# A new table of issue order, engines and TensorE fillers for an attention-and-feed-forward kernel on one Trainium2 core

## The chip, the core and the metric

The kernel runs on one core of a Trainium2 chip. A core has five instruction streams, each strictly in order: TensorE (PE, with its weight loads shown apart as PEld), VectorE (DVE), ScalarE (ACT), GpSimd (POOL) and SyncE (SP), which issues nearly all DMAs. [...] The metric is the device time of one execution in microseconds; the time before is 741.42 us, the median of three runs (740.2 to 742.83).

## The reference

Attention over 4 batches, 8 heads, 576 positions and 64 dimensions a head, with a bias that a small network makes from the relative position (the same for all batches), and then a two-layer feed-forward part on the 2304 x 512 result.

```python
scores = scale * np.matmul(q, k.transpose(0, 1, 3, 2))
x = (psi_rel / psi_i)[..., None]               # log1p(|i-j|) / log1p(max(i,1))
bias = np.maximum(x @ w1 + b1, 0.0) @ w2       # 32 hidden units, 8 heads
attn = softmax(scores + bias)                  # over the last axis
out = np.matmul(attn, v)                       # -> x of (B*S, H*D) = (2304, 512)
h = x @ w_in                                   # d_ff = 2048
g = np.maximum(h, 0.0) + alpha * np.minimum(h, 0.0)
return g @ w_out
```

## The kernel before, in words

The program is made in two steps. First the functions below record 2816 work items, each with its engine alternatives (an item may be able to run on ACT, DVE or POOL), its operands and its buffers. Then `plan` reads three tables of numbers. `ISSUE` gives the order in which the items are issued, and behind a dot the alternative that each takes (`58.2` is item 58 on its third alternative). `SLOT` gives the buffer of each tile. `IDLE` (`62:24`) says that 24 fillers stand ahead of item 62: matmuls of 512 columns on zeros into the tile `H`, which nobody reads (L995). Nothing is decided at run time: each engine runs its items in the table's order, and an item that has to wait holds up all that stands behind it on its engine. The framework sets the semaphores from the tiles that the items touch, in the table's order.

What runs, in time:

- **Bias tiles** (`bias_tile`, 36 of them, until about 130 us). Four "H" items each make max(R*sign + psi, 0) on 128 partitions and 304 to 576 columns, on ACT (L479), DVE (L476) or POOL (L482). PE multiplies them with `w2b` into PSUM (L497), one item scales the result into `fg` (L507 or L508), and SP writes it to DRAM (`scr`).
- **Weights** (`weights`, 8 pairs of blocks, mixed with the bias tiles). DVE puts 32-bit halves together (L667, L670), takes a maximum (L674), and both weights are split into a high and a low 16-bit part (L695, L696, L689, L690, and L388 on DVE for the low part). Two tiny PE transposes (L458, L460) spread each maximum over all partitions.
- **Attention units** (`unit`, 64 of them). SP loads the bias rows into `fg`; PE makes scores (L602 in 32 bits for batch 0, L603 in three 16-bit products for batches 1 to 3); DVE adds the bias and takes the row extremum (L797); ACT exponentiates (L800); the sums are inverted (L803, L805). In batch 0 the rows are then scaled (L820 on POOL, L821 on DVE) and turned on PE (L829, copied back by L839 or L840). In batches 1 to 3 a high part (item "nh", L810 on POOL or L811 on ACT) and a low part (L813 on DVE) go into one of two `a` buffers, and two DMA transposes on SP write them to `at`. PE multiplies with v (L850, L858), and ACT and DVE write the two parts of `x` (L876, L878).
- **Feed-forward chunks** (`chunk`, `layer_pair`; 9 chunks of 256 rows, 8 pairs of hidden blocks each, from 195.7 us on). The first layer is 24 matmuls (L928) into the one `H` buffer; ACT (L935) and DVE (L936) apply the activation; item "g0" (L939) and item "g1" (L940 on DVE, L941 on POOL) split the result; the second layer is 12 matmuls (L947) that add up in PSUM tile `O`, one half for each 128 rows. The last pair of a group issues the two halves of `O` as two PE items of six matmuls, and each half is then evicted (item "mo", L909 on ACT or L910 on DVE; L913 on DVE where four groups are added up, in chunks 0 and 1).

The lines around the fillers are:

```python
    gaps = {int(n): int(k) for n, k in (x.split(":") for x in IDLE.split())}
    with tc.manual_schedule():
        for o in ordered:
            for _ in range(gaps.get(o.seq, 0)):
                nc.tensor.matmul(idle, lhsT=zero.broadcast_to((P, P)), ...)
            o.alt()
```

## Time and profile before

| | |
|---|---|
| median of three runs | 741.42 us |
| the profiled execution | 740.16 us, span 738.3 us (first to last instruction) |
| PE busy | 678.8 us (92%), 5712 matmuls |
| DVE busy | 534.7 us (72%) |
| ACT busy | 366.5 us (50%) |
| POOL busy | 239.8 us (32%) |
| mean granted PE clock | 0.988 |

Until 195.7 us no feed-forward matmul runs; this stretch is called the first stage below, the rest the second. Busy time is the union of an engine's instructions; PE's includes the fillers. In the first nine of the page's forty slices PE stands at 7 to 8 tenths mostly and DVE at 9, and from slice 11 on PE stands at 9 and DVE at 6 to 8. PE's clock is granted in full from about 160 us on.

### The profile page before, as it was taken

The page shows a single profiled execution, that of the slowest core. Times are in us where ns is not written, and L with a number is a line of the kernel's source. Part 1 is how long each engine was busy: PE and PEld are TensorE (multiplying, and loading weights), DVE is VectorE, ACT ScalarE, POOL GpSimd, SP SyncE. Part 2 cuts the span into 40 slices and gives each one's busy share as a digit, 9 for nine tenths or more (in the row PEclk, how much of TensorE's full clock was granted, in tenths as well). Part 3 has the DMA queues.
Part 4 walks back from the last instruction along what each step waited for, and adds up shares of the span by engine and source line. Part 5 has one row for each costly group of instructions (what it writes and reads, how often), then busy time and mean ns, then how long its engine had stood idle before and what let it go on. Part 6 is the DMA issues. An engine that isn't in the chain of part 4 may idle for free. (4 is left out here: it accounts for less than half of the span.)

```text
span 738.3 us, 15339 instructions
## 1 busy us (share of the span) xinstructions
PE 678.8 (92%) x5712; PEld 425.4 (58%) x5712; DVE 534.7 (72%) x1228; ACT 366.5 (50%) x753; POOL 239.8 (32%) x297
## 2 busy tenths in 40 slices
PE   7777779787999989998999999999999999999997
PEld 3444334444665656665667565656666666666764
DVE  6999899999687879898778766767676656333322
ACT  3556657566565547664465564544454534211221
POOL 2556677523122313233322232224223232110110
PEclk9999989899999999999999999999999999999999
DMA  8897875773849888999999998788789965400000
GB/s 204 212 285 258 257 278 183 243 207 120 211 107 229 177 185 174 218 209 223 194 229 199 173 206 177 163 194 211 138 178 199 193 143 84 68 29 1 29 1 29
DMA packets 236554, 125.89 MB, mean 171 GB/s; under 512 B 204864, under 2 KB 204864, under 8 KB 236480
## 3 DMA queue, kind: packets, MB, share of 16 engines
q1 hardware_dynamic: 233840, 124.90, 72.3%
q8 instruction: 45, 0.74, 0.4%
q10 hardware_dynamic: 2640, 0.01, 0.2%
q14 instruction: 29, 0.24, 0.1%
HBM read 73.87 MB, written 15.61 MB: 121 GB/s over the span
## 5 line engine op out<-in xcount | busy, mean ns | idle before, releaser
L947 PE MATMUL O<-wout,mg 128*128 128x512 f16 x864 | 199.0, 379 | 8.4 <-DVE mg L910 3.4
L928 PE MATMUL H<-x,win 128*128 128x256 f16 x1728 | 200.7, 273 | 2.8 <-DVE mg L936 2.7
L928 PEld LDWEIGHTS <-win 128*128 128x128 f16 x1728 | 166.8, 98 | 35.0 <-issue 8.5
L935 ACT ACTIVATE mg<-H,sm 128x256 f32<-128x256 f32 x144 | 65.0, 471 | 155.7 <-PE H L928 122.5
L947 PEld LDWEIGHTS <-mg 128*128 128x128 f16 x864 | 82.1, 98 | 103.3 <-issue 13.7
L800 ACT ACTIVATE fg<-fg,st 128x576 f32<-128x576 f32 x144 | 110.8, 770 | 59.7 <-DVE st L797 52.1
L936 DVE SCALAR_TENSOR_TENSOR mg<-H,sm,mg 128x256 f32<-128x256 f32 x144 | 67.0, 480 | 95.6 <-ACT mg L935 95.1
L813 DVE SCALAR_TENSOR_TENSOR a<-fg,st,a 128x576 f16<-128x576 f32 x108 | 97.9, 909 | 26.6 <-POOL a L810 16.1
L810 POOL TENSOR_SCALAR a<-fg,st 128x576 f16<-128x576 f32 x74 | 59.9, 811 | 175.3 <-DMA at<-a 72.9
L941 POOL TENSOR_TENSOR mg<-mg 128x512 f16<-128x512 f32 x48 | 61.2, 1275 | 151.6 <-DVE mg L939 51.1
L797 DVE CUSTOM_DVE_ANT_0 fg<-S,fg 128x576 f32<-128x576 f32 x127 | 93.4, 749 | 20.6 <-PE S L603 19.7
L482 POOL TENSOR_SCALAR at<-cst,npsi 128x496 f32<-128x496 f32 (+16 forms) x66 | 56.2, 860 | 45.7 <-PE S L497 30.2
L497 PE MATMUL S<-at,w2b 128*32 128x79 f32 (+37 forms) x684 | 54.4, 355 | 15.7 <-POOL at L482 7.0
L603 PE MATMUL S<-qk 64*128 64x288 f16 (+1 forms) x678 | 52.8, 285 | 1.2 <-DVE st L797 0.9
L497 PEld LDWEIGHTS S<-at,w2b 128*32 128x32 f32 x684 | 26.3, 114 | 46.0 <-POOL at L482 18.5
L850 PE MATMUL A<-at,five 128*64 128x256 f16 (+3 forms) x720 | 51.6, 288 | 0.0
L603 PEld LDWEIGHTS <-qk 64*128 64x128 f16 (+1 forms) x720 | 32.1, 96 | 23.7 <-issue 18.1
L850 PEld LDWEIGHTS <-five 128*64 128x64 f16 (+1 forms) x720 | 36.1, 109 | 14.5 <-issue 11.3
L803 POOL TENSOR_SCALAR st<-st 128x2 f32<-128x2 f32 (+1 forms) x42 | 13.3, 316 | 80.2 <-ACT fg L800 70.3
L811 ACT ACTIVATE a<-fg,st 128x576 f16<-128x576 f32 x34 | 26.3, 773 | 14.3 <-DMA at<-a 4.9
L820 POOL TENSOR_SCALAR fg<-fg,st 128x576 f32<-128x576 f32 x29 | 24.9, 864 | 24.2 <-DVE st L805 12.9
L479 ACT ACTIVATE at<-cst 128x576 f32<-128x576 f32 (+16 forms) x39 | 24.8, 655 | 15.8 <-PE S L497 11.5
(148 smaller groups left out, 825.9 us busy)
## 6 DMA issues: line engine op xcount, KB each, us to landing
fg<-scr SPq DMA_DIRECT2D x64, 576.0 KB, 4.7
scr<-fg SPq DMA_DIRECT2D x36, 295.5 KB, 4.4
x<-in_moe_w_in_dram SPq DMA_DIRECT2D x10, 512.0 KB, 5.7
x<-in_moe_w_out_dram SPq DMA_DIRECT2D x10, 512.0 KB, 4.5
fg<-scr SPq DMA_DIRECT2D x32, 144.0 KB, 4.5
out_dram<-mg SPq DMA_DIRECT2D x18, 256.0 KB, 2.9
five<-in_q_dram SPq DMA_DIRECT2D x32, 128.0 KB, 4.3
five<-in_k_dram SPq DMA_DIRECT2D x32, 128.0 KB, 4.0
```

The lines of the kernel that those rows point to most:

```text
L497: nc.tensor.matmul(ps.t[32 * gl:32 * gl + 32, c:n], lhsT=w2b, rhs=x, start=True, stop=True)
L603: return [(lambda a, dst=dst, zq=zq, zk=zk, i=i: nc.tensor.matmul(dst(a), lhsT=tr16(qt)[at, 0, pr, zq, lo:lo + n], rhs=tr16(qt)[at, 1, pr, ...
L797: V(lambda x=x, sl=sl, st=st, ls=ls: nc.vector.tensor_tensor_reduce(out=in_halves(ls[x]()), in0=halves(sl[x].t), in1=in_halves(ls[x]()), s ...
L800: A(lambda x=x, st=st, ls=ls: nc.scalar.activation(ls[x](), ls[x](), AF.Exp, bias=st.t[:, x:x + 1], scale=-1.0, accum_out=st.t[:, 2 + x:3 ...
L810: pl.op([("POOL", 775, lambda x=x, rec=rec, ls=ls, a16=a16: nc.gpsimd.tensor_scalar(a16.t[:, 0:S], ls[x](), rec(), 1.0, op0=ALU.mult, op1= ...
L813: V(lambda x=x, rec=rec, ls=ls, a16=a16: nc.vector.scalar_tensor_tensor(a16.t[:, 640:640 + S], ls[x](), rec(), a16.t[:, 0:S], op0=ALU.mult ...
L850: nc.tensor.matmul(ps.t[64 * hh:64 * hh + 64, 0:w], lhsT=v5[0:hi, zv, n, 2 * pr + hh, :], rhs=at16(at)[0:hi, 5 * za + n, 320 * hh:320 * hh ...
L928: nc.tensor.matmul(hb.t[:, f, :], lhsT=win[:, fp, zw, kb, P * f:P * f + P], rhs=x[:, zx, kb, :], start=(n == 0), stop=(n == 11))
L935: A(lambda f=f: nc.scalar.activation(gf(f), hb.t[:, f, :], AF.Copy, scale=cu[:, f:f + 1]), 470, ky, [hb, t_sig], [(g, f)])
L936: V(lambda f=f: nc.vector.scalar_tensor_tensor(gf(f), hb.t[:, f, :], cs[:, f:f + 1], gf(f), op0=ALU.mult, op1=ALU.max), 475, ky, [hb, t_si ...
L941: ("POOL", 1210, lambda: nc.gpsimd.tensor_tensor(gv(1), g.t, gv(0), op=ALU.subtract))], ky, [g, (gg, 0)], [(gg, 1)], tag="g1", cont=True)
L947: nc.tensor.matmul(ob.t[:, t, :], lhsT=gg.t[:, zg, f, P * t:P * t + P], rhs=wout[:, fp, zw, f, :], start=(first and f == 0 and (zg, zw) == ...
```

## The change

Only `ISSUE` and `IDLE` differ; the items, their arithmetic, the buffers (`SLOT`) and all code stay. The file is one line shorter, so every line number behind the tables is lower by one in the kernel after (L947 is L946 there).

```diff
 ISSUE = """
-11.1 15.1 3 9.1 0 203 2 12.1 1 204 205 206 17 14.1 8.1 5.1 19 20 21 22 24 6.1 23 25 29 58.2 59.2 61.1 16.1 207 80.2 13.1 10.1 7.1 33 26 60 62 208 209
...
+3 5.1 0 203 2 8.1 1 207 11.1 17 14.1 12 15.1 6.1 16.1 7.1 204 205 9.1 206 13.1 208 10.1 209 18.1 210 215 219 33 211 19 20 21 22 24 34 23 25 29 26 58
...
 IDLE = """
-62:24 118:1 111:2 683:3 97:3 655:2 132:2 641:1 676:3 957:1 139:3 634:1 697:1 160:3 669:2 146:2 725:2 704:3 711:1 753:1 739:2 746:3 569:2 767:2 560:1
-353:1 580:2 596:2 614:1 806:9 814:3 793:2
+30:23 62:2 118:2 90:1 104:1 111:2 683:2 55:3 97:3 132:1 641:2 676:4 959:1 662:1 139:2 634:2 697:1 160:2 669:4 718:5 725:4 704:1 711:1 739:7 388:1
+569:3 549:2 767:1 563:1 353:3 596:3 611:1 800:1 419:1 614:1 806:2 814:8 828:4 796:2
```

Counted in the two tables, 289 of the 2816 items run on another engine:

| items | before | after |
|---|---|---|
| on DVE / ACT / POOL / SP | 1084 / 602 / 293 / 423 | 1101 / 658 / 219 / 424 |
| H on ACT / DVE / POOL | 43 / 29 / 72 | 72 / 36 / 36 |
| nh on POOL / ACT | 74 / 34 | 65 / 43 |
| g1 on POOL / DVE | 48 / 24 | 33 / 39 |
| mo on DVE / ACT | 10 / 8 | 5 / 13 |
| of those that the first L928 item hangs on: DVE / ACT / POOL | 330 / 167 / 124 | 343 / 205 / 75 |
| fillers | 91 | 111 |
| places on PE where the tile shape of one item differs from the last | 318 (193 from the first L928 item on) | 324 (188) |

The row on the first L928 item counts the items that must be done before it: those that it depends on through data and buffers, and those that stand ahead of these on their engines. On PE the order moves little: 258 of the 414 items keep their place in the row, and none moves by more than five. All fillers stand in the first stage in both.

Three places show what moved. The first is DVE's start of the program, where L667, L670 and L674 belong to the first weight block, L422 to L426 scale the small network's first weights, and L427 to L432 prepare the constants that every H item reads. Before:

```order
L667 TENSOR_SCALAR win<-mg 128x512
L670 SCALAR_TENSOR_TENSOR win<-mg,win 128x512 x2
L422 TENSOR_REDUCE sm<-sm 128x1
L423 TENSOR_SCALAR sm<-sm 128x1
L424 RECIPROCAL sm<-sm 128x1
L425 TENSOR_TENSOR sm<-sm 128x1
L427 TENSOR_SCALAR cst<-cst,sm 128x576
L426 TENSOR_TENSOR sm<-sm 128x1
L428 TENSOR_SCALAR cst<-cst,sm 128x144
L432 TENSOR_SCALAR npsi<-cst 128x144
L476 TENSOR_SCALAR at_85<-cst 128x560
L429 TENSOR_SCALAR w2b<-w2b,sm 128x32
```

After:

```order
L666 TENSOR_SCALAR win<-mg 128x512
L669 SCALAR_TENSOR_TENSOR win<-mg,win 128x512 x2
L666 TENSOR_SCALAR win<-x_93 128x512
L669 SCALAR_TENSOR_TENSOR win<-x_93,win 128x512 x2
L673 TENSOR_REDUCE sm<-win 128x1
L421 TENSOR_REDUCE sm<-sm 128x1
L422 TENSOR_SCALAR sm<-sm 128x1
L423 RECIPROCAL sm<-sm 128x1
L424 TENSOR_TENSOR sm<-sm 128x1
L426 TENSOR_SCALAR cst<-cst,sm 128x576
L425 TENSOR_TENSOR sm<-sm 128x1
L427 TENSOR_SCALAR cst<-cst,sm 128x144
```

The second half of the first weight block (`x_93`) and its maximum now stand ahead of the small network's chain, and the H item (L476) behind it has gone. In the table SP's load of the constants has moved behind the load of `x_93`, and one of ACT's small loads is now issued by SP.

The second place is ACT in the first bias tiles (L479 and L478 are H items, L507 and L506 the scaling of a finished tile, L675 and L674 a weight's maximum). Before:

```order
L479 ACTIVATE fg<-cst 128x512
L479 ACTIVATE at_85<-cst 128x432
L507 ACTIVATE fg<-S_64,cst 128x591
L479 ACTIVATE at_85<-cst 128x432
L507 ACTIVATE fg<-S_65,cst 128x591
L507 ACTIVATE fg<-S_64,cst 128x591
L675 ACTIVATE wout,sm<-wout 128x1024
L479 ACTIVATE at_85<-cst 128x544
L479 ACTIVATE fg<-cst 128x400
L507 ACTIVATE fg<-S_64,cst 128x591
```

After:

```order
L478 ACTIVATE at_85<-cst 128x560 x2
L478 ACTIVATE fg<-cst 128x512
L478 ACTIVATE at_85<-cst 128x512
L506 ACTIVATE fg<-S_64,cst 128x591
L478 ACTIVATE at_85<-cst 128x432 x3
L478 ACTIVATE at_85<-cst 128x496
L478 ACTIVATE fg<-cst 128x496
L478 ACTIVATE at_85<-cst 128x496
L506 ACTIVATE fg<-S_65,cst 128x591
L674 ACTIVATE wout,sm<-wout 128x1024
```

Between two scalings there stood no more than two H items, and now up to six stand there; their counterparts have left POOL.

The third place is the end of the program on PE: the weight load and matmul that end the first half of the last chunk's `O`, and the start of the second half, with the semaphores that each waits for. Before:

```order
L947 LDWEIGHTS mg
L947 MATMUL O_63<-wout,mg 128x512
L947 LDWEIGHTS mg
L947 MATMUL O_63<-wout,mg 128x512 [waits DVE_49]
L947 LDWEIGHTS mg
```

After:

```order
L946 LDWEIGHTS mg
L946 MATMUL O_63<-wout,mg 128x512
L946 LDWEIGHTS mg
L946 MATMUL O_63<-wout,mg 128x512
L946 LDWEIGHTS mg
```

The eviction of the first half stood ahead of the second half's matmuls in the table and stands behind them now, and the wait for it has gone. In the same way an eviction stood between two halves in seven places before; in four of these nothing but the eviction stood between them for PE. Now it does so in two places (chunk 1, groups 0 and 1), with other PE items between.

## Rows read from the trace of the kernel before

**Rows 1.** Windows: length, busy us (count) of PE, PEld, DVE, ACT, POOL, PEclk, DMA.
```profile
0.00:20.00 20.00, 15.12 (x116) 7.19 (x116) 12.81 (x32) 7.21 (x9) 6.74 (x12) 0.91 0.87 201
20.00:180.00 160.00, 126.82 (x1209) 67.47 (x1208) 151.42 (x298) 97.12 (x169) 91.23 (x110) 0.96 0.73 230
180.00:196.00 16.00, 15.02 (x113) 9.13 (x112) 11.16 (x37) 8.18 (x20) 4.98 (x7) 1.00 0.79 196
196.00:560.00 364.00, 348.54 (x2974) 227.51 (x2973) 281.66 (x689) 199.56 (x436) 106.07 (x139) 1.00 0.90 189
560.00:738.30 178.30, 173.25 (x1310) 114.11 (x1306) 77.65 (x174) 54.44 (x122) 30.83 (x31) 1.00 0.35 74
```

**Rows 2.** Timeline of 4.5 to 13.5 us, DVE and POOL: start, length, idle before.
```profile
4.55 0.43 DVE L667 TENSOR_SCALAR win<-mg 128x512 int32<-128x512 int32 x1 [2.27 <-DMA mg<-in_moe_w_in_dram]
5.01 1.42 DVE L670 SCALAR_TENSOR_TENSOR win<-mg,win 128x512 int32<-128x512 int32 x2
...
8.24 0.15 DVE L422 TENSOR_REDUCE sm<-sm 128x1 f32<-128x1 f32 x1 [1.81 <-DMA sm<-in_w_dram]
...
10.32 1.62 POOL L482 TENSOR_SCALAR at<-cst,npsi 128x560 f32<-128x560 f32 x2 [9.88 <-DVE npsi L432]
...
11.92 0.95 POOL L482 TENSOR_SCALAR fg<-cst,npsi 128x512 f32<-128x512 f32 x1
...
12.34 1.07 DVE L670 SCALAR_TENSOR_TENSOR win<-x,win 128x512 int32<-128x512 int32 x1
```

**Rows 3.** Durations by line, ns min/median/max: L670, L482, L479, L476.
```profile
L670 DVE SCALAR_TENSOR_TENSOR five<-x,five x22: 680/693/1486, 96.2 to 173.6; 128x512 int32<-128x512 int32 x22
...
L482 POOL TENSOR_SCALAR at<-cst,npsi x66: 517/764/2063, 10.3 to 126.7; 128x544 f32<-128x544 f32 x5, 128x464 f32<-128x464 f32 x5, 128x384 f32<-128x384 f32 x5, 128x560 f32<-128x560 f32 x4
...
L479 ACT ACTIVATE at<-cst x39: 537/651/779, 10.0 to 129.3; 128x576 f32<-128x576 f32 x4, 128x416 f32<-128x416 f32 x4, 128x432 f32<-128x432 f32 x3, 128x544 f32<-128x544 f32 x3
...
L476 DVE TENSOR_SCALAR at<-cst x24: 373/494/929, 10.1 to 115.2; 128x496 f32<-128x496 f32 x3, 128x400 f32<-128x400 f32 x3, 128x480 f32<-128x480 f32 x3, 128x384 f32<-128x384 f32 x2
```

**Rows 4.** Windows of one line each, first stage: L670 and L476 (DVE), L482 (POOL).
```profile
0.00:196.00 196.00, 53.40 (x64) 0.96 0.75 225
...
0.00:196.00 196.00, 17.21 (x29) 0.96 0.75 225
...
0.00:196.00 196.00, 61.59 (x72) 0.96 0.75 225
```

**Rows 5.** Waits of PE from 196 us: in total, times, longest (us).
```profile
PE O L947 <- DVE mg L910: 3.4, 3, 1.8
PE H L928 <- DVE mg L936: 2.7, 4, 1.0
PE O L947 <- DVE mg L913: 2.0, 1, 2.0
```

**Rows 6.** Timeline where an eviction stands between two halves of `O`.
```profile
269.55 0.74 DVE L913 SCALAR_TENSOR_TENSOR mg<-O,sm,mg 128x512 f32<-128x512 f32 x1
...
270.35 1.46 PE L947 MATMUL O<-wout,mg 128*128 128x512 f16 x6 [2.00 <-DVE mg L913]
...
416.95 1.46 PE L947 MATMUL O<-wout,mg 128*128 128x512 f16 x6 [1.75 <-DVE mg L910]
...
732.98 1.46 PE L947 MATMUL O<-wout,mg 128*128 128x512 f16 x6 [0.84 <-DVE mg L910]
```

**Rows 7.** Timeline of PE: a first layer before another shape, and before its own.
```profile
586.59 2.79 PE L928 MATMUL H<-x,win 128*128 128x256 f16 x24
589.32 0.92 PE L603 MATMUL S<-qk 64*64 64x288 f16 x12
...
657.06 2.78 PE L928 MATMUL H<-x,win 128*128 128x256 f16 x24
659.68 2.54 PE L947 MATMUL O<-wout,mg 128*128 128x512 f16 x11
```

**Rows 8.** What POOL's "nh" items (L810) waited for: us, times.
```profile
  DMA at<-a: 72.9, 27
```

183 rows, old and new, of the table ISSUE are left out of this document.

## The prediction

> **What bounds the kernel now.** I read the windows by stage first [rows 1], then the start of the timeline [rows 2], then durations by line [rows 3], and for the later part the waits of PE [rows 5]. From 20 to 180 us DVE is busy for 151.42 of 160 us, while PE has 126.82, ACT 97.12 and POOL 91.23: in the first stage everybody waits for DVE, so this stage is priced as DVE's. From 196 us on it is the other way round: PE is busy for 348.54 of 364 us and then for 173.25 of 178.3, DVE for 281.66 of 364 (77%). There only what keeps PE from its next matmul counts. The reader is to see that PE's whole idle time from 196 us on is 15.5 + 5.0 us, and 33.2 us from 20 to 180.
>
> **First stage: DVE beside POOL.** The same instruction of DVE has two lengths. At 5.01 us two L670 take 1.42 us, 0.71 each, and POOL has nothing to do yet; at 12.34 one L670 takes 1.07 us, and POOL runs an H item of 0.95 us that began at 11.92 [rows 2]. Over the run L670 goes from 680 to 1486 ns [rows 3]. In the first stage its 64 instructions take 53.40 us [rows 4] against 64 x 0.68 = 43.5: 9.9 us are lengthening. For L476 (29 H items on DVE, 17.21 us) the widths differ, so I bound it: 29 x 0.494 (the median) leaves 2.9 us of lengthening, 29 x 0.373 (the shortest) leaves 6.4; I take 4.6, the middle. Of DVE's other lines that read SBUF I show no row; I put 1.5 us for them, and 16 us in all. POOL, which does this, is busy for 6.74 + 91.23 + 4.98 = 103 us in this stage. The change takes 49 of 124 items off it, 36 of them H items at 61.59 / 72 = 0.855 us [rows 4]; pricing all 49 so, 41.9 us of 103 go. In proportion DVE gets back 16 x 41.9 / 103 = 6.5 us. The ends are 0 (what is left of POOL stands in the way as often) and 16 (nothing meets any more).
>
> [...]
>
> **First stage: work that comes to DVE.** Of the items that the first L928 hangs on, DVE has 13 more. Seven are H items at 0.494 us [rows 3]: 3.5 us. The other six are the net of likes that come and go; between nothing and six mean instructions of this stage (175.4 us / 367 = 0.48, so 2.9 us) [rows 1]. I take 1.5; together +5.0 us.
>
> **First stage: the start.** Before, DVE waits for the first weight half (2.27 us) and then for the small network's weights (1.81 us, until 8.24) [rows 2]. Now the second weight half stands in that gap: one L667 and two L670 more (0.43 + 1.42 = 1.85 us) and a maximum, which I price at two L670 (1.42). So when the chain of L422 begins, at about 4.55 + 2 x 1.85 + 1.42 = 9.7 us instead of 8.24, DVE is 3.3 us of work ahead; the H items begin 1.4 us later. Net 1.8 us gained, about the 1.81 us of the gap. It needs the constants by then: SP's load of them now waits until the first weight half has landed (4.55 us), so it has 5 us; if it lands later, this term falls to 0. The small load that moves from ACT to SP waits behind that, and is needed at the same time.
>
> First stage: -6.5 + 5.0 - 1.8 = **-3.3 us**. Three things I cost at nothing. ACT takes 38 items more, 29 of them H items at 0.651 us [rows 3] (18.9 us): it has 62.9 us idle between 20 and 180 us; if that cover is gone it is a rival below. The 20 fillers more run in PE's 33.2 us of idle time. And SP's other loads only change places with neighbours.
>
> **Second stage: the evictions between two halves.** PE's longest waits there are not for data. The second half of a chunk's last item waits for the eviction of the first half, which stands ahead of it in the table: 3.4 us in three waits for L910 and 2.0 us in one for L913 [rows 5], at 270.35 (2.00), 416.95 (1.75), 732.98 and one more (0.84 each) [rows 6]. At 269.55 one sees why the first is so long: L913 itself starts late, since DVE does other work first. In the new order none of the four has an eviction between: -5.4 us. The 0.84 us at the end is sure, as nothing but the last eviction follows. For the others something is late next: behind the one at 270 the score item that reuses `O`'s bank has both evictions ahead of it (0 to 0.74 us; I take 0.5). The two places where an eviction now stands between have cover: in chunk 1, group 1, a whole first layer (2.6 us), so nothing; in group 0 only twelve score matmuls (0.92 us [rows 7]) and a small pair against an eviction of 0.74 us and what DVE has ahead of it: 0 to 2.0, the longest wait seen; I take 0.6. Together +1.1.
>
> **Second stage: changes of tile shape.** A first layer of 24 matmuls is followed after 589.32 - 586.59 = 2.73 us by another shape and after 659.68 - 657.06 = 2.62 us by its own [rows 7]: 0.11 us a change. From the first L928 on there are 188 changes instead of 193: -0.5 us. (In the first stage there are 11 more, mostly around fillers; PE has time there.)
>
> **Second stage: the rest.** 15 of the g1 items net go from POOL to DVE, 9 of the nh items net from POOL to ACT, and 5 evictions from DVE to ACT. These lie beside PE while it has work; I cost them at nothing. PE's idle time from 196 to 560 us without the three waits there (4.6 us) is 10.9 us, and half of it either way is what they could do.
>
> Second stage: -5.4 + 1.1 - 0.5 = **-4.8 us**. In all -8.1 us. The profiled execution took 740.16 us (span 738.3 and 1.9 around it), so 732.1 by its measure; it lies 1.3 us under the median of the runs, 741.42, from which the forecast is **733.3 us**.
>
> **Rivals.**
> - *DVE and POOL hardly meet any more.* The term is 16 instead of 6.5 us: 723.8 us. For it speaks that the table was made with both in view; against it, that POOL keeps 36 H items and DVE is busy for 95% of the time. 0.08.
> - *ACT becomes what the first stage waits for.* With 38 items more at about 0.65 us it is busy for some 122 of 160 us, in order, and up to six H items now stand ahead of the scaling of a finished tile. If that eats the first stage's gain, 736.6 us. 0.13.
> - *The four waits come back.* PE arrives earlier and waits for DVE at the next item, as it did for L936 already (2.7 us in four waits [rows 5]); only the last 0.84 us stay: 737.9 us. 0.09.
> - *Nothing moves.* 258 of PE's 414 items keep their place, and what DVE loses in lengthening it gets back as work (5.0 of 6.5 us); the rest drowns in other waits: about 741 us. 0.12.
> - *ACT stalls on the `a` buffers: slower.* POOL waited 72.9 us in 27 waits for the DMA transposes that free them [rows 8], 2.7 us each, 27 of 74 items. POOL could afford it. Now 24 such items come to ACT (15 go back). If the same share waits, that is 8.8 waits of 2.7 us, with L935 queued behind them on ACT, and L935 empties the only `H` buffer, for which PE's next first layer waits. PE has one second layer as cover, so a stall costs between 0 and 2.7 us; at the middle, 1.35, it is 11.9 us: 745.2 us. It decides from six such stalls on (8.1 / 1.35). Against it: ACT is idle for 45% of 196 to 560 us [rows 1], so an item that waits there need not hold up much. 0.16.
>
> **How the numbers follow.** The forecast itself has 0.42. About 0.3% (2.2 us) is what a measurement of this kernel can tell from no change. Faster by more: the forecast and the first three rivals, 0.72. Within: 0.12. Slower: 0.16. The range goes from the first rival, 723, to 744, which takes in the second, third and fourth, half of the other idle time either way, and about half of the last.
>
> **What would show it.** Right: L670 in the first stage falls from 53.4 us to 46 to 51; the first L928 starts 2 to 6 us before 195.7; no wait of L947 for L910 of 0.8 us or more is left, and the last halves of `O` follow each other at once. Wrong: ACT above 85% between 20 and 180 us and DVE under 90%, which is the second rival; ACT's L811 idle behind DMA transposes for more than 10 us and PE's first layers waiting for L935 or L936 for more than 8 us, which is the last; new waits of PE right behind 270 and 417 us, which is the third.

## The result and the profile after

The kernel after takes **711.56 us** (median of four runs, 710.6 to 713.04) against 742.12 us for the kernel before, measured beside it (740.2 to 742.88): 0.959 of the time, with an interval of 0.957 to 0.962. That is 30.6 us less, where the forecast had 8.1 less and a range down to 723. The direction was right, two terms were far too small. In the runs below line numbers can be one or two lower than in the kernel before (L928 is L927 or L926, L670 is L669 or L668); the text uses the numbers of the kernel before where it says nothing else.

The first reading is where the 28.8 us between the two profiled spans (738.3 and 709.5) lie. The first L927 starts at 179.08 us instead of 195.74, so 16.7 us come from the first stage and 12.1 us from behind it. Windows of the kernel before and then of the kernel after, split at the first layer's first matmul (columns as in [rows 1]):

```profile
0.00:195.74 195.74, 156.70 (x1432) 83.55 (x1433) 175.34 (x365) 112.25 (x195) 102.94 (x128) 0.96 0.75 225
195.74:738.30 542.56, 522.05 (x4282) 341.86 (x4279) 359.37 (x863) 254.27 (x560) 136.90 (x169) 1.00 0.72 151
```

```profile
0.00:179.08 179.08, 153.09 (x1453) 81.10 (x1453) 159.37 (x375) 136.02 (x235) 56.54 (x80) 0.98 0.83 247
179.08:709.50 530.42, 519.90 (x4282) 341.83 (x4279) 354.32 (x871) 261.40 (x575) 111.17 (x143) 1.00 0.74 154
```

In the first stage DVE runs ten instructions more and is busy for 16 us less; its idle time (20.4 and 19.7 us) has not changed. So its instructions have become shorter. L669, DVE's 64 instructions answering to L670, takes 44.83 us in the first stage (window of that line alone) against 53.40 [rows 4]. Two of its six groups, the largest, which is in [rows 3], and the one with the longest median, read so (the second first as it was before, minimum, median and maximum in ns):

```profile
0.00:179.08 179.08, 44.83 (x64) 0.98 0.83 247
```

```profile
L670 DVE SCALAR_TENSOR_TENSOR wout<-mg,wout x8: 684/822/1124, 17.6 to 89.5; 128x512 int32<-128x512 int32 x8
...
L669 DVE SCALAR_TENSOR_TENSOR five<-x,five x22: 674/691/1096, 88.0 to 158.1; 128x512 int32<-128x512 int32 x22
...
L669 DVE SCALAR_TENSOR_TENSOR wout<-mg,wout x8: 669/692/693, 16.7 to 82.2; 128x512 int32<-128x512 int32 x8
```

For all of DVE I use one measure below, called **lengthening**: for each DVE instruction, its duration in the trace less the usual one of its line, operation and shape (the 20th percentile over all kernels told of here), summed over the instructions that start before the first layer's first matmul, or behind it. A POOL instruction is said to lie beside a DVE instruction if it overlaps it, and the one with the longest overlap counts. In the first stage the lengthening goes from 23.7 to 4.9 us, while the usual durations of what DVE does sum to 170.4 and 174.6 us. (Together they are some 19 us more than DVE's busy time, since neighbouring instructions overlap in the trace; so a change of the sum need not be the same change of the busy time.)

Behind the first stage PE is busy nearly as long as before (522.05 and 519.90 us), and its idle time falls from 20.5 to 10.5 us, of which 3.9 and 4.6 us lie behind its last instruction. PE's waits there (total, times, longest):

```profile
PE H L927 <- DVE mg L935: 1.2, 2, 0.7
PE S L576 <- DVE st L796: 1.0, 1, 1.0
PE O L602 <- DVE mg L912: 0.9, 1, 0.9
PE O L946 <- DVE st L796: 0.8, 1, 0.8
```

The waits of the second layer for an eviction, 5.4 us in [rows 5], are not in the list any more, and the wait of the first layer has gone from 2.7 to 1.2 us.

### The profile page after: what moved, and what is told of

Its sections match the earlier page's. It is cut to its first block, busy times and chain, and to the rows that moved or that the text cites. A ratio compares the mean times of both kernels' runs of the same rounds, so it can differ in the third digit from the quotient of the medians.

```text
span 709.5 us, 15371 instructions
## 1 busy us (share of the span) xinstructions
PE 673.0 (95%) x5732; PEld 422.9 (60%) x5732; DVE 513.7 (72%) x1245; ACT 397.4 (56%) x809; POOL 167.7 (24%) x223
## 4 chain that ended last, share of the span: by engine, by line
PE 71%; DVE 18%; issue 4%; DMA 3%; ACT 2%; POOL 1%; ACTq 0%; SPq 0%; DVEq 0%; POOLq 0%
PE H L927 25%; PE O L946 24%; PE S L602 6%; PE A L849 6%; DVE five L669 3%; DVE fg L796 3%; PE A L857 2%; PE S L496 2%; PE S L828 2%; PE S L576 2%; PE S L601 1%; DMA at<-a 1%; DVE wout L387 1%; DVE mg L935 1%; DVE fg L507 1%
## 5 line engine op out<-in xcount | busy, mean ns | idle before, releaser
L927 PE MATMUL H<-x,win 128*128 128x256 f16 x1728 | 200.7, 273 | 1.3 <-DVE mg L935 1.2
L946 PE MATMUL O<-wout,mg 128*128 128x512 f16 x864 | 198.7, 379 | 1.6 <-DVE st L796 0.8
L927 PEld LDWEIGHTS <-win 128*128 128x128 f16 x1728 | 166.6, 98 | 34.0 <-issue 7.1
L946 PEld LDWEIGHTS <-mg 128*128 128x128 f16 x864 | 82.0, 98 | 95.1 <-issue 6.5
L934 ACT ACTIVATE mg<-H,sm 128x256 f32<-128x256 f32 x144 | 62.3, 469 | 135.4 <-PE H L927 121.0
L935 DVE SCALAR_TENSOR_TENSOR mg<-H,sm,mg 128x256 f32<-128x256 f32 x144 | 64.8, 478 | 101.0 <-ACT mg L934 100.7
L812 DVE SCALAR_TENSOR_TENSOR a<-fg,st,a 128x576 f16<-128x576 f32 x108 | 90.0, 834 | 21.0 <-POOL a L809 16.1
L809 POOL TENSOR_SCALAR a<-fg,st 128x576 f16<-128x576 f32 x65 | 54.1, 834 | 177.2 <-DMA at<-a 70.1
L940 POOL TENSOR_TENSOR mg<-mg 128x512 f16<-128x512 f32 x33 | 41.2, 1247 | 157.4 <-ACT mg L938 68.1
L496 PE MATMUL S<-at,w2b 128*32 128x79 f32 (+35 forms) x684 | 50.1, 345 | 8.3 <-ACT fg L506 3.4
L849 PEld LDWEIGHTS <-five 128*64 128x64 f16 (+1 forms) x720 | 36.0, 109 | 14.7 <-issue 11.3
L478 ACT ACTIVATE at<-cst 128x464 f32<-128x464 f32 (+17 forms) x62 | 39.1, 658 | 8.0 <-PE S L496 4.5
L810 ACT ACTIVATE a<-fg,st 128x576 f16<-128x576 f32 x43 | 32.9, 769 | 18.6 <-DMA at<-a 11.3
L481 POOL TENSOR_SCALAR at<-cst,npsi 128x416 f32<-128x416 f32 (+15 forms) x32 | 24.9, 785 | 58.0 <-PE S L496 33.2
L994 PE MATMUL H<-sm 128*128 128x512 f16 x111 | 33.5, 412 | 0.9 <-DVE w2b L405 0.9
L819 POOL TENSOR_SCALAR fg<-fg,st 128x576 f32<-128x576 f32 x29 | 23.2, 808 | 44.6 <-DVE st L804 24.6
```

The source lines that it names most:

```text
L496: nc.tensor.matmul(ps.t[32 * gl:32 * gl + 32, c:n], lhsT=w2b, rhs=x, start=True, stop=True)
L809: pl.op([("POOL", 775, lambda x=x, rec=rec, ls=ls, a16=a16: nc.gpsimd.tensor_scalar(a16.t[:, 0:S], ls[x](), rec(), 1.0, op0=ALU.mult, op1= ...
L812: V(lambda x=x, rec=rec, ls=ls, a16=a16: nc.vector.scalar_tensor_tensor(a16.t[:, 640:640 + S], ls[x](), rec(), a16.t[:, 0:S], op0=ALU.mult ...
L849: nc.tensor.matmul(ps.t[64 * hh:64 * hh + 64, 0:w], lhsT=v5[0:hi, zv, n, 2 * pr + hh, :], rhs=at16(at)[0:hi, 5 * za + n, 320 * hh:320 * hh ...
L927: nc.tensor.matmul(hb.t[:, f, :], lhsT=win[:, fp, zw, kb, P * f:P * f + P], rhs=x[:, zx, kb, :], start=(n == 0), stop=(n == 11))
L934: A(lambda f=f: nc.scalar.activation(gf(f), hb.t[:, f, :], AF.Copy, scale=cu[:, f:f + 1]), 470, ky, [hb, t_sig], [(g, f)])
```

## The experiments

All in one table: median, start of the first layer, DVE's lengthening up to there, and the span behind it. The kernel before stands first, the kernel after second. The last three columns are read from the one profiled execution of each kernel; it lies within 2.3 us of the median, but for e13 (715.90 us, 2.7 above) and e14 (750.69 us, 3.5 above).

| kernel | median us | first L928 at | lengthening to there | behind it |
|---|---|---|---|---|
| before | 742.1 | 195.74 | 23.7 | 542.6 |
| after | 711.6 | 179.08 | 4.9 | 530.4 |
| e1 before, POOL's H items write zeros | 733.0 | 186.05 | 15.5 | 542.8 |
| e2 after, old fillers | 720.1 | 186.84 | 5.5 | 530.8 |
| e3 before, new engines | 820.4 | 247.18 | 9.7 | 572.7 |
| e4 after, old engines | 735.7 | 196.56 | 18.6 | 537.4 |
| e5 after, old fillers, own start | 716.1 | 183.59 | 4.8 | 530.5 |
| e6 after, no fillers but the start | 713.2 | 182.81 | 5.2 | 530.2 |
| e7 before, evictions moved | 736.9 | 195.87 | 23.1 | 539.4 |
| e8 new first stage, old rest | 723.7 | 179.11 | 4.9 | 543.1 |
| e9 after, old POOL engines behind | 715.7 | 179.23 | 4.8 | 535.1 |
| e10 after, old DVE and ACT engines behind | 716.1 | 180.23 | 4.9 | 534.5 |
| e11 after, 29 H items back on POOL | 721.5 | 189.93 | 13.3 | 531.2 |
| e12 after, DVE's start filled | 711.2 | 179.28 | 5.8 | 530.2 |
| e13 after, H items swapped in a tile | 713.2 | 182.73 | 7.5 | 531.4 |
| e14 before, no fillers but the start | 747.2 | 202.18 | 24.7 | 546.5 |

### Do the two stages add up? (e8)

Up to the first L928 this is the kernel after, from there the kernel before.

The table begins with the first 924 items of the kernel after, with the first L928 (item 2181) next in line; what is left follows in the order and on the engines of before. At the seam, in the kernel after's table:

```diff
 983 891.1 2179.1 984 883 1045
-2181 901 1009 903 985 986
+481 2190 901 903 2181 892
```

> A splice: up to the first L928 the order, engines and all fillers of the kernel after, from there the order and engines of the kernel before. If the two stages add up, as their first L928 and their rest do in the traces (195.7 to 179.1 us, and 17.4 to 7.2 us of PE idle behind it), the first L928 comes at 178 to 181 us and the time is 724 to 727 us. If the second stage gained by starting with more of its work prepared (rival), part of its 12 us comes along and the time is below 721 us; if the old second stage needs the old engines' state at the seam, it is above 728 us.

Measured: 723.65 us, 0.975 (0.972 to 0.978) of before. Its windows:

```profile
0.00:179.11 179.11, 153.91 (x1453) 82.56 (x1454) 159.56 (x375) 135.84 (x235) 57.17 (x80) 0.98 0.83 247
179.11:722.20 543.09, 523.36 (x4282) 342.05 (x4279) 359.36 (x862) 252.79 (x559) 137.69 (x168) 1.00 0.72 150
```

The first row is the kernel after to 0.1 us, the second the kernel before to 0.6 us. The time is 0.35 us below the range that was expected if the stages add up, and both rivals fall. The stages add up, and can be explained apart.

### First stage: the price of POOL beside DVE (e1, e11)

e1 takes the suspected cost away and leaves POOL its items; only these H items, and with them the bias, compute something else:

```diff
-                nc.gpsimd.tensor_scalar(hb.t[:, 0:wd], R[:, 0:wd], 3.0e38, npsi[:, g:g + 1], op0=ALU.min, op1=ALU.max)
+                nc.gpsimd.memset(hb.t[:, 0:wd], 0.0)
```

> The kernel before, with one line changed: the H items that run on POOL write zeros into their buffer (a memset of the same width) instead of reading the constants; the bias is therefore wrong, and nothing else is left out. POOL keeps its 72 items and its place in the order, but these no longer read SBUF. Theory 1 (the first stage of the kernel before is long because DVE's instructions are lengthened by POOL's beside them): the 22 us or so by which DVE's instructions are longer than their usual length before the first L928 fall to under 8 us, the first L928 starts 10 to 16 us before 195.7 us, and the time is 725 to 732 us. Rival A (the lengthening is there but the stage is set by the order of the items and by what ACT takes over): the lengthening falls, but the first L928 starts within 4 us of 195.7, and the time stays above 737 us. Rival B (a write of POOL holds DVE up as a read does): the lengthening stays above 15 us and so does the time, about 741 us.

Measured: 732.99 us, 0.989 (0.987 to 0.991). The lengthening falls by 8.2 us and the first L928 comes 9.7 us earlier, while the span behind it stays. All three figures of theory 1 were missed (the lengthening of 15.5 us is even what rival B, a write that holds DVE up as a read does, had asked for), but the stage did get shorter with the lengthening, which rivals A and B excluded. Why the fall is smaller is seen beside the instructions (e1, timeline of DVE and POOL):

```profile
39.29 1.19 POOL L696 TENSOR_SCALAR win<-win,sm 128x1024 f16<-128x1024 f32 x1
39.53 1.48 DVE L670 SCALAR_TENSOR_TENSOR wout<-mg,wout 128x512 int32<-128x512 int32 x1
...
47.28 0.81 DVE L476 TENSOR_SCALAR at<-cst 128x480 f32<-128x480 f32 x1 [1.53 <-PE S L497]
47.33 1.20 POOL L482 MEMSET at<- 128x480 f32 x2 [6.12 <-PE S L497]
...
69.17 1.42 DVE L670 SCALAR_TENSOR_TENSOR win<-x,win 128x512 int32<-128x512 int32 x2
69.55 0.78 POOL L482 MEMSET at<- 128x416 f32 x2 [1.57 <-PE S L497]
```

At 69.17 two L670 beside two memsets keep their 0.71 us each. At 39.53 one L670 beside POOL's L696, which reads SBUF, takes 1.48. At 47.28 an L476, which has one SBUF input, takes 0.81 us beside a memset (0.46 is usual for its 480 columns). Counted over the first stage: of 17 L670 that lie beside a memset none is lengthened by more than 0.06 us, where in the kernel before 14 of the 20 beside a reading H item are; of 12 L476 beside a memset 9 are, 14 of 23 before. What lies beside POOL's other items costs as much as before (9.0 and 8.5 us), and the H items' part falls from 12.8 to 5.0 us. The memsets are also shorter than the items they replace (34.03 us in all, against 61.59 in [rows 4]), so part of this fall is their length; what says that reading matters is the L670.

How much an L670 loses can be read too. In the kernel before 24 of the 64 take more than 0.75 us. Every one of them starts while a POOL instruction runs, and ends 0.54 us (0.536 to 0.547) after that instruction ends; one that is not held up takes 0.69. (At 12.34 us in [rows 2] the H item ends at 12.87 and the L670 at 13.41; above, L696 ends at 40.48 and the L670 at 41.01.) So what it loses is what is left of POOL's instruction when it starts, less some 0.15 us. Of all DVE instructions of the first stage of before that take over 0.1 us more than usual, 60 of 60 start during one of POOL's, and they hold some 21.6 us of the lengthening. The reverse does not hold: of the 28 L670 that start so, 4 keep their length (0.70 us or less).

A rival for e1 is that PE no longer waits for POOL's H items: 7.0 us in six waits before, 0.9 in two waits in e1. But DVE's idle time, where such a wait would have to show, is the same (20.4 and 20.8 us); what falls is DVE's busy time, from 175.34 to 165.25 us:

```profile
PE S L497 <- POOL at L482: 7.0, 6, 2.3
...
0.00:186.05 186.05, 150.40 (x1432) 82.36 (x1433) 165.25 (x365) 111.69 (x195) 74.54 (x128) 0.96 0.80 237
```

e11 goes the other way, in the kernel after: 29 H items go from ACT to POOL (eight of them shown).

```diff
 ISSUE = """
-58 80 79 114 68 100 680 93
+58.2 80.2 79.2 114.2 68.2 100.2 680.2 93.2
```

> The kernel after, with those 29 H items that went from POOL to ACT put back on POOL; the order and everything else stay. ACT has some 19 us less to do in the first stage, POOL some 22 us more, DVE the same. Theory 1: each H item on POOL costs DVE between 0.05 us (as the 36 in the kernel after do) and 0.18 us (as the 72 before did), so DVE's lengthening in the first stage rises from 5 to between 6.5 and 10 us, the first L928 comes 1.5 to 6 us later and the time is 713 to 718 us. Rival A (ACT is what now holds up the first stage): the time falls below 710 us.

Measured: 721.54 us, 10.0 us above the kernel after, outside both expectations. ACT is relieved and DVE has the same items as in the kernel after, and yet DVE is busy for 167.79 instead of 159.37 us up to the first L928:

```profile
0.00:189.93 189.93, 160.01 (x1452) 84.32 (x1453) 167.79 (x375) 120.53 (x206) 80.75 (x109) 0.96 0.78 233
```

The lengthening rises by 8.4 us, which is 0.29 us for each of the 29 items, more than the mean of the 72 before (12.8 us / 72 = 0.18). And 8.4 us of lengthening go with 10.9 us of first stage; in e1 8.2 us went with 9.7. That is no price of lengthening alone: in e1 DVE's busy time fell by 10.1 us with its idle time unchanged, and in e11 the idle time rises by 2.4 us, with PE waiting 5.0 us for POOL's H items (L481) instead of 1.1.

### First stage: number or place? (e3, e4, e13)

e3 and e4 exchange order and engines between the two kernels, for all 289 items. e3 is the kernel before with the new engines, for instance in the first bias tile:

```diff
 ISSUE = """
-58.2 59.2 61.1
+58 59.2 61
```

> The kernel before, its order and fillers, with the engines of the kernel after for all 289 items that change engine. If the amount of work on POOL decides (128 POOL instructions before the first L928 become about 80), DVE's lengthening in the first stage falls from 22 to 8 us or less and the time is 715 to 725 us. If it is the place in time of what POOL keeps, which needs the new order, the lengthening falls only in proportion to POOL's work (83 to 48 us), to about 13 us, and the time is 730 us or more, or above 741 where the old order doesn't fit the new engines.

e4 is the kernel after with the old engines:

```diff
 ISSUE = """
-58 60.2 61 80 82.2
+58.2 60 61.1 80.2 82
```

> The kernel after, its order and fillers, with the engines of the kernel before for all 289 items. If the amount of work on POOL decides, DVE's lengthening in the first stage is back at 18 us or more, the first L928 comes at 192 us or later, and only part of the gain after it (evictions, tile shapes) stays: 727 to 740 us. If the place in time decides, the lengthening is 12 us or less and the first L928 comes before 187 us.

e3 takes 820.44 us, 79 more than before and far more than the figures of either theory (the second had allowed for more than 741 if the old order doesn't fit the new engines), with a lengthening of 9.7 us between theirs, and says little on its question: DVE idles for 81.3 us of the first stage, 26.1 of it in 12 waits of its H items for a buffer that PE frees with L497. Engines and order are fitted to one another: the new engines in the old order are worse than either kernel. e4 takes 735.66 us, 0.992 (0.991 to 0.994): with POOL's 72 H items back the lengthening is 18.6 us, as the theory of amount had it, and the first stage gains nothing, although the lengthening is 5.1 us below that of before: DVE's idle time is 26.5 us instead of 20.4. So the lengthening alone does not set the stage; where this idle time comes from no run here separates.

```profile
0.00:196.56 196.56, 162.62 (x1453) 86.60 (x1453) 170.07 (x364) 113.17 (x196) 102.38 (x130) 0.95 0.75 225
196.56:734.00 537.44, 520.87 (x4282) 342.27 (x4279) 355.31 (x865) 249.25 (x558) 132.00 (x167) 1.00 0.73 152
```

One difference at the same number of POOL items is seen in one group: the scaled rows of batch 0 (L820) cost 3.8 us of lengthening in the kernel before with 27 items on POOL, 1.6 in e4 with the same 27. The H items cost 12.8 us in both. So the order's part lies beside POOL's other items (L820, L696, L690): 9.0 us before, some 4 in e4, and some 1.5 in the kernel after.

e13 keeps number, widths and order of the kernel after: in 29 pairs of H items of the same bias tile, the one on POOL and the one on ACT exchange engines (three pairs shown).

```diff
 ISSUE = """
-58 60.2 61 59.2 82.2 79
+58.2 60 61.2 59 82 79.2
```

> The kernel after, with 29 of the 36 H items on POOL exchanged with an H item of the same bias tile that ran on ACT: POOL, ACT and DVE have as many H items as before, of the same widths, tile by tile; order and fillers stay. If the amount on POOL decides, DVE's lengthening in the first stage stays at 5 to 6 us and the time at 710.5 to 713.5 us. If the place decides (in the kernel after only 11.4 of the 27.7 us of POOL's H items lie beside those kinds of DVE instruction that are seen to be lengthened, in the kernel before 44.8 of 62.3 us), the lengthening rises to 7 us or more, about half of the way to 0.18 us per item, and the time is 714 us or more.

Measured: 713.22 us (711.98 to 715.9), lengthening 7.5 us, first L928 at 182.73 us: by the time it reads as amount, by the lengthening as place. The 182.73 us come from the slowest of the four executions and say less than the median. The lengthening is clear: eight kernels here share engines and order of the first stage with the kernel after, but for fillers and two moved DVE items, and have 4.8 to 5.8 us. So both are at work. 29 items at another place cost 2.6 us of lengthening, 29 items more cost 8.4 (e11). In the kernel before 44.8 of the 62.3 us of POOL's H items lie beside those lines of DVE that are seen to be lengthened, in e13 18.1 of 30.7 and in the kernel after 11.4 of 27.7 (beside L670 and L476 alone 27.8, 12.7 and 5.0). How far the larger of the two, the number, would go with the best places, no run here separates.

### The fillers (e2, e5, e6, e14)

All four change `IDLE` alone. e2, the kernel after with the old table:

```diff
 IDLE = """
-30:23 62:2 118:2 90:1 104:1 111:2 683:2
+62:24 118:1 111:2 683:3
```

> The kernel after, with the 91 fillers of the kernel before in their places instead of its own 111; order and engines stay. Theory 1 (DVE and POOL): the fillers matter little, 710 to 714 us, and the first L928 stays within 2 us of 179.1. Rival C (the new fillers keep PE's clock up; before, the granted clock was 0.86 to 0.97 from 80 to 160 us, in the kernel after 1.00 from 20 us on): the clock falls below 0.95 in several 20 us windows of the first stage and the time is 716 us or more.

e5, the old table behind the new start:

```diff
 IDLE = """
-30:23 62:2 118:2 90:1 104:1 111:2 683:2
+30:23 62:2 118:1 111:2 683:3
```

> The kernel after with its own 25 fillers at the start (ahead of items 30 and 62) and, for the rest, the 67 fillers of the kernel before in their places, instead of its own 86. In the run with all the old fillers the 24 of the start stood behind PE's first real item, since that is item 30 in the new order, and kept PE's bias matmuls back by several us; here that is mended. Theory 1 (DVE and POOL carry the first stage's gain): 710 to 714 us, the first L928 within 2 us of 179.1. Rival C (the new fillers and PE's clock carry part of it): 717 us or more, as in that run (720.1), with the granted clock below 0.95 in several windows of 20 us between 80 and 180 us.

e6, the new start alone:

```diff
 IDLE = """
-30:23 62:2 118:2 90:1 104:1 111:2 683:2
+30:23
```

> The kernel after without any filler but the 23 ahead of item 30. This prices the fillers in all. Theory 1: PE is not what the first stage waits for, so a lower clock costs little, below 5 us: 711 to 717 us. Rival C: the granted clock falls to 0.5 to 0.8 in the stretches where PE waits, its bias matmuls take up to twice as long there, and the time is 722 us or more.

e14, the kernel before with its start alone:

```diff
 IDLE = """
-62:24 118:1 111:2 683:3 97:3
+62:24
```

> The kernel before without its 67 fillers behind the start (the 24 of the start stay). If the fillers pay by keeping PE's clock up, as the placed ones of the kernel after do (1.6 us), the time is 743 us or more. If fillers that stand in the wrong place cost more than they give, as the old ones did in the new order (716.1 us against 713.2 without), the time is 740 us or less.

e2 measured 720.14 us, but for a reason of its own: the 24 fillers of the start stand ahead of item 62, and PE's first real item in the new order is 30, which runs at 12.29 us (11.76 in the kernel after, with 23 fillers ahead of it), so PE did nothing until then (7.71 us busy in the first 20). e5 mends that and takes 716.09 us, e6 713.20 us. So the 88 fillers of the kernel after behind the first 23 are worth 1.6 us against none (710.6 to 713.04 against 712.59 to 714.83, barely clear), and the old 67 in the new order, with two new ones at the start, cost 2.9 us. From the old places to the new ones, in the new order, it is 4.5 us (e5 against the kernel after). In the kernel before the same 67 are worth 6 us: without them 747.17 us, 1.008 (1.005 to 1.011), as the first of e14's two expectations had it. The windows of 80 us in the middle of the first stage, of e14, of the kernel before and of the kernel after:

```profile
80.00:160.00 80.00, 59.94 (x522) 32.26 (x514) 76.71 (x145) 47.85 (x85) 51.81 (x55) 0.85 0.70 235
```

```profile
80.00:160.00 80.00, 65.02 (x552) 34.40 (x542) 77.30 (x150) 49.39 (x87) 48.92 (x55) 0.91 0.73 239
```

```profile
64.00:144.00 80.00, 66.75 (x650) 35.18 (x651) 77.55 (x166) 66.73 (x118) 30.24 (x36) 1.00 0.86 283
```

The granted clock is 0.85, 0.91 and 1.00, and DVE is busy for 96 to 97% in all three: a slower PE costs DVE only what it then waits for PE (idle time of DVE in the first stage 25.1 us in e14, 20.4 before). Rival C of these expectations, that the new fillers carry the gain, falls: without them 28.9 of 30.6 us are still there (e6). But e2 and e5 lie above theory 1's 714 too, so the places of the fillers do matter. The clock was rival C's sign, and came: 0.91 in three windows of 20 us between 100 and 180 us in e2, 0.88 and 0.86 in two between 140 and 180 us in e5. Yet in e6 it is 0.86 to 0.92 in all five windows from 80 to 180 us, and e6 is 2.9 us faster than e5. So the old fillers cost more in the new order than the clock that they keep up gives back. This loss I put down to fillers that stand ahead of a matmul that is ready; no run here shows that by itself. A clock as low as e6's rival had it shows in short stretches of the kernel before (0.50 from 139 to 145 us, where one L829 follows the other on PE after 0.21 us instead of the 0.11 at full clock, both medians), but no window of 20 us of e6 from 20 us on has less than 0.86.

### Second stage: evictions and engines (e7, e9, e10)

e7 moves four PE items in the kernel before, and nothing else (three of the four shown):

```diff
-2248 2251 1384.1 1391.1 2253 1144.1 1145 1158 1146 2249 2252
+2248 2249 2251 1384.1 1391.1 2253 1144.1 1145 1158 1146 2252
...
-2397 2399.1 2396
+2397 2396 2399.1
...
-2741 2743.1 2745 2742
+2741 2742 2743.1 2745
```

> The kernel before with four PE items moved: where the eviction of the first half of O stood between two halves with nothing else of PE (270, 417, 483 and 733 us), the second half now stands right behind the first. Engines and all else stay. The prediction's step: the four waits, 5.4 us, go and 0.5 come back, so 4.9 us less, about 736.7 us, and no wait of L947 for L910 of 0.8 us or more is left. Rival (the waits come back at the next item that needs DVE): less than 2 us gained, 739.5 us or more.

Measured: 736.87 us, 0.992 (0.989 to 0.996); its span behind the first L928 is 3.2 us shorter, the medians differ by 5.2. Waits of PE from 196 us on (its lines are one lower, as in the kernel after):

```profile
PE H L927 <- DVE mg L935: 3.1, 5, 1.0
PE S L828 <- DVE qk L583: 1.3, 2, 0.9
PE O L602 <- DVE mg L912: 1.1, 1, 1.1
```

The waits for L910 and the 2.0 us one for L913 of [rows 5] are gone and little comes back. The price of this step was right within what the two readings leave open (3.2 to 5.2, forecast 4.9). e4, which has the whole new order and the old engines, is 5.1 us shorter behind its first L928 than the kernel before: this is put down to the order. The other 7.0 us need the new engines, and e9 and e10 take these back in two groups, in the kernel after: e9 for the 105 items of the second stage that can run on POOL, e10 for the 49 that DVE and ACT share (the first few of each shown).

```diff
 ISSUE = """
-910 907 2187 2199 932.1
+910.1 907.1 2187.1 2199.1 932
```

> The kernel after, with the engines of the kernel before for the items nh, g1, ep, z and no of the second stage alone (105 items; those that can run on POOL). The first stage and the rest stay. The new order with all the old engines had 5.1 us less behind the first L928 than the kernel before (534.3 against 539.4), the kernel after has 12.3 us less (527.1); so the second stage's engines are worth 7.2 us, which the prediction costed at nothing. Theory X (it is POOL beside DVE again: DVE's lengthening there is 17.6 us before and 10.1 after): most of the 7.2 us is lost, the rest takes 532 us or more, DVE's lengthening there is 14 us or more and the time is 716 to 720 us. Theory Y (it is the evictions and g0 that went from DVE to ACT): the time stays at 711 to 713 us.

```diff
 ISSUE = """
-893.1 912.1 923 2198.1 2206 2191.1
+893 912 923.1 2198 2206.1 2191
```

> The kernel after, with the engines of the kernel before for the items g0, mo, at and mq of the second stage alone (49 items; those that DVE and ACT share). Theory X (POOL beside DVE): 711 to 713 us, DVE's lengthening in the second stage stays at 9 to 11 us. Theory Y (evictions and g0 on ACT bring it): the rest behind the first L928 takes 531 us or more and the time is 715 to 719 us.

Measured: 715.70 and 716.11 us, so 4.1 and 4.6 us above the kernel after. e9 shows theory X's signs (the span behind, and the lengthening given below; its time is 0.3 us under that theory's range), e10 shows theory Y's, so both hold in part. Their spans behind the first layer are 4.7 and 4.1 us longer, together more than 7.0: they do not simply add up.

```profile
179.23:714.30 535.07, 520.92 (x4282) 342.49 (x4279) 350.74 (x855) 255.11 (x566) 132.96 (x168) 1.00 0.74 153
```

```profile
180.23:714.70 534.47, 520.39 (x4282) 342.03 (x4279) 358.59 (x878) 256.20 (x568) 109.26 (x143) 1.00 0.74 153
```

In e9 DVE has less to do than in the kernel after (350.74 against 354.32 us busy), and yet PE waits longer: DVE's lengthening there is 15.7 us instead of 10.0, 7.0 of it beside POOL's g1 items (3.1 in the kernel after, 9.7 in the kernel before). In e10 the lengthening is 11.4 us, and DVE has 4.3 us more of ordinary work, which ACT had taken; POOL's part is as in the kernel after. In both PE's first layer waits longer for the activation on DVE (2.2 us in e9 and 3.2 in e10, against 1.2).

### The start (e12)

```diff
-467 468 63 81.1 39 27 117.1 83 469 114 40 217
+467 217 218 468 63 81.1 39 27 117.1 83 469 114
```

> The kernel after with two DVE items moved: the two L669 (0.7 us each) of the first block of the second weights stand right behind L705 instead of behind the first three H items, in the 2.90 us in which DVE waits at 12.8 us for PE to free a buffer. The prediction priced the start at 1.8 us gained; the trace of the kernel after has more idle time of DVE there than before. If the first stage is DVE's from the start, this gives 1.4 us or nearly: 709.8 to 710.8 us. If what DVE is ahead at the start is lost at the next wait for PE (20.7 or 24.6 us), the time stays at 711 to 712 us.

Measured: 711.23 us (710.3 to 711.86), no difference that this measurement can tell, and the first L928 0.2 us later. DVE's waits for PE (L497, L495 there) up to 40 us fall from 5.2 to 3.2 us and nothing follows from it; the lengthening up to the first L928 is 0.9 us more (5.8; the others with this first stage have 4.8 to 5.5). Where the gain goes stays open. No version here is shown to beat the kernel after.

## Why the prediction was right and wrong

**Direction and mechanism** were right, the sizes of the signs to look for were not: L670 was to fall to between 46 and 51 us and fell to 44.83, the first L928 was to come 2 to 6 us earlier and came 16.7. As forecast, DVE bounds the first stage and POOL lengthens its instructions, PE bounds the rest, and the waits of L947 for L910 and L913 are gone. How POOL lengthens L670 is seen in all 24 that are long: each ends 0.54 us after the POOL instruction that ran when it started. The prediction showed one beside an H item [rows 2]; the three longest (1.41 to 1.49 us) stand beside L696, a longer item of POOL (1.27 to 1.52 us).

**The contention term is the step that failed.** "In proportion DVE gets back 16 x 41.9 / 103 = 6.5 us" measured 18.8 us (23.7 to 4.9). Two things in it were too small. The sum of 16 us: L670 at 9.9 us was right (9.4), H items on DVE 4.6 (4.9), but "DVE's other lines", put at 1.5 us without a row, hold some 9. And the proportion: it took all of POOL's items for equal and their place for given. Of the 18.8 us some 11 lay beside the H items and some 7.5 beside POOL's other items, of which few left; there it is the order that counts (e4). Put back in the new order 29 of the H items that left cost 0.29 us each (e11), more than the mean of 0.18 before, and those that stayed stand less beside the instructions that are lengthened (e13). The rival that contention is wholly gone, held at 0.08, was the nearest for this stage: it has 12.8 us of first stage (16 + 1.8 - 5.0) against 16.7 measured. Its 723.8 us and the 723.65 of e8 agree by chance, since the rival's number holds 4.8 us of second stage and e8 holds none. Of the 16.7 us e11 takes back 10.9 and e5 4.5, each by itself in the new order; what is left no run separates.

The items can be sorted by what the runs show, where the prediction took a mean. Beside POOL's memsets 0 of 17 L670 and 9 of 12 L476 are lengthened (e1), beside its reading H items 14 of 20 and 14 of 23 (kernel before). L797, which has its scores in PSUM, is not seen to be lengthened by POOL at all: it takes 729 to 758 ns in 127 instructions, 60 of which lie beside one of POOL (kernel after). How near a price by such a sorting would have come no run shows.

```profile
L796 DVE CUSTOM_DVE_ANT_0 fg<-S,fg x127: 729/750/758, 71.4 to 588.9; 128x576 f32<-128x576 f32 x127
```

**Work that comes to DVE**, +5.0 forecast, measured 174.6 - 170.4 = 4.2 us: right.

**The start**, -1.8 forecast, gave nothing. Moving the second weight half ahead fills the gap of 1.81 us in [rows 2], but the maximum (L673) then stands ahead of the chain too, which begins at 9.57 instead of 8.24 us, near the forecast 9.7. What the term had not in it is that behind the chain DVE's H items wait for a buffer:

```profile
8.44 1.22 DVE L673 TENSOR_REDUCE sm<-win 128x1 f32<-128x1024 f32 x1
9.57 0.14 DVE L421 TENSOR_REDUCE sm<-sm 128x1 f32<-128x1 f32 x1
...
12.64 0.17 DVE L705 TENSOR_REDUCE sm<-sm 128x1 f32<-128x16 f32 x1
15.71 0.49 DVE L475 TENSOR_SCALAR at<-cst 128x512 f32<-128x512 f32 x1 [2.90 <-PE S L496]
```

Up to 40 us DVE is busy for 28.91 us and was for 31.78; its usual work done by then is the same (31.1 and 30.9 us), since the lengthening is 3.4 us less. In e12 2.0 us less of these waits bring nothing by 179 us.

**The fillers**, costed at nothing, are worth 4.5 us in the new order from the old places to the new ones (e5), against no fillers behind the start 1.6 us in the kernel after (e6) and 6 us in the kernel before (e14). That they run in "PE's 33.2 us of idle time" was not enough as a reason: without them PE's items take longer at the lower clock (up to the first L928, besides fillers, they keep PE busy for 146 us in e14 at a clock of 0.86, and for 132 us before at 0.96), and DVE's idle time in the first stage rises from 19.7 to 23.2 us (e6) and from 20.4 to 25.1 us (e14).

**Evictions and tile shapes**, -4.8 us for the second stage: the new order alone gives 5.1 us (e4), the evictions alone 3.2 to 5.2 (e7). Right in sum; the 0.5 us for the tile shapes no run tests by itself.

**"The rest", costed at nothing**, is the second failure: the engines of the second stage give 7.0 us (e4 against the kernel after; e9 and e10, each alone, 4.7 and 4.1 us of span). The prediction's cover was that these items lie beside PE while it has work, with half of 10.9 us of idle time either way; 7.0 is beyond that half. It read PE's waits for DVE as given, and did not ask why DVE is late: it is late because POOL lengthens it (15.7 us in e9, 10.0 in the kernel after) and because it does what ACT can do (4.3 us of usual work in e10).

**The rivals of the other side.** ACT did take on the work, and is busy for 136.02 of 179.08 us in the first stage, without becoming its bound. The stall on the `a` buffers came as often as the rival had it, 10 waits instead of 8.8, but at 1.1 us each instead of 2.7 (11.3 us in all), and PE's first layers wait for 1.2 us in all, where the rival had 11.9: its cover was nearly whole, not half. No rival and no end of the range came near 711.6.

```profile
ACT a L810 <- DMA at<-a: 11.3, 10, 2.9
```

## What to carry to other kernels

Where one engine lengthens another's instructions, do not price the items that leave by their share of the busy time: sort both engines' instructions into those that meet and those that do not (here L670 is lengthened beside 14 of 20 reading H items and beside 0 of 17 memsets), and count which overlaps go: what an L670 loses here is the rest of POOL's instruction at its start, less 0.15 us (24 of 24). An item put back cost 0.29 us (e11) where the share of busy time gave 0.13 (16 / 124). Work that lies beside the bounding engine is not free if the engine that feeds it is late for the same reason (7.0 us here, e4 against the kernel after). And a table of engines and a table of order are one thing: exchanging one alone cost 79 us (e3) or lost four fifths of the gain (e4).

## What the runs showed of the hardware

- POOL writing zeros does not lengthen L670, which has two SBUF inputs (0 of 17), and does lengthen L476, which has one (9 of 12; 0.81 us for 480 columns against a usual 0.46). Reading H items lengthen both (14 of 20 and 14 of 23).
- An L670 that is held up ends 0.54 us (0.536 to 0.547) after the POOL instruction that ran when it started, in 24 of 24 cases of the kernel before's first stage; by itself it takes 0.69 us.
- Without fillers behind the start the granted clock of the kernel before falls to 0.85 between 80 and 160 us (0.91 with them), and what PE does up to the first L928 besides fillers keeps it busy for 146 us instead of 132 (one execution of each; that of e14 is 3.5 us above its median).
